# Streamed key and value weight pieces: one load per row piece instead of two half loads

## The chip, the cores and the metric

The kernel runs on one core of a Trainium2 chip. The metric is the device time of one execution in microseconds: the median of three runs before is 3,844.53 us (3,838.34 to 3,846.89). The profiled execution has a span of 3,837.5 us, from which all times below are taken. Engines are called PE (TensorE, matrix products; its weight loads are a row of their own, PEld), DVE (VectorE), ACT (ScalarE), POOL (GpSimd) and SP (SyncE, which here only issues transfers). Transfers from SP share one load queue, q1; those from POOL go through q0.

## The reference

Four layers, A B A B, act on `x` of 2048 rows and 640 columns, all bf16. Only layer A matters here; it is a recurrence over segments:

```python
for s in range(n_seg):                       # 64 segments of 32 rows
    h = concatenate([mem, xs])               # 8 memory rows + 32 rows of x
    q, k, v = h @ Wq, h @ Wk, h @ Wv         # 640 -> 32 heads x 192 each
    p = softmax(where(mask, q @ k.T * scale, -1e9))
    o = (p @ v) @ Wo                         # 6144 -> 640
    mem = o[:8]                              # goes into the next segment
    outs.append(o[8:])
```

The segments must run one after the other, since the first 8 output rows of one are the first 8 input rows of the next. Layer B is a linear attention with softmax features, and each layer adds its result to `x`. Layer A runs twice, so there are 128 segments.

## The kernel before, in words

**Where the weights are.** Each of Wq, Wk and Wv is 640 x 6144. It is cut in 4 rounds of 1536 columns (8 heads each; `PW = 1536`) and in 5 contraction blocks of 128 rows (`KC = 5`), which makes 20 pieces of 128 partitions x 1536 columns, 384 KB each. Not all of it fits in the on-chip memory beside the output weight Wo. So of each matrix 17 places are held: rounds 1 and 2 whole, two blocks of rounds 0 and 3 each for good (`res`), and three places (`SLOTS`, `slot`) that blocks 2, 3 and 4 of rounds 0 and 3 use in turn. The rounds of a segment run 0, 1, 2, 3 in even segments and 3, 2, 1, 0 in odd ones (`rounds`), so what the last round of a segment used is what the first round of the next one needs. Per segment each slot is loaded once. Wo has the same trouble: rounds 1 and 2 stay in `wo_mid`, rounds 0 and 3 share `wo_end`, which is loaded with six pieces of 320 KB in each segment (`load_wo`, line 625; they come from `wo_rows`, a copy of these rounds with contiguous rows).

**A segment.** `A_chain` (lines 811 to 1095) writes out by hand the order of all instructions (a manual schedule). For each of the four rounds there are query, key and value projections (`project`, line 867, matmuls of line 882, 20 for each projection), scores (lines 919, 924), softmax sums (985), the attention product (`attend`, 932), and the round of the output projection (`wo_round`, 48 matmuls of line 958, which reads the six Wo pieces one after the other, 8 matmuls each). The four rounds' work is interleaved: the projections of a round come ahead of the attention of the one before it. The output projection of the last round ends the segment; lines 1091 and 1092 turn its first rows into the columns `hT` that the next segment's first matmuls read.

**When the slots are loaded.** In the first round (`n == 0`) `project` starts with the blocks in the slots, and right after the four matmuls of such a block it puts the load of the last round's block in the slot:

```python
b = (i + KC - ns) % KC if n == 0 else i
...
if n == 0 and b >= KC - ns:
    load_slot(m, order[NR - 1], b)
```

The load has to wait until those matmuls have read the slot, and its data is used in the last round, block by block. Queries come first, then keys, then values. The Wo pieces are issued after the first `wo_round` of the segment has read `wo_end`.

**How the matmuls read a piece.** Matmuls of one block come in four, one for each group `g` of 32 output partitions. For keys and queries each of the four reads columns from all over the piece, in strides. For values each reads 384 neighbouring columns, in the order of groups 0, 2, 1, 3 of the columns, so the first and third lie in the first half of the piece and the second and fourth in the second half.

**Queue.** SP issues all these loads in the program's order and waits in front of each for what it needs; a later load can't pass an earlier one. Eight semaphores count the landings of SP's loads in turn, so each load also waits until the eighth load before it has landed. POOL issues small transfers at the same time: the tails of keys and queries (`load_kqb`, line 853) and values (`extra_v`, line 865) that were worked out ahead, and results (lines 834, 849, 951).

**Ahead of the chain.** `A_pre` works out those tails for all segments; there `load_matrix` calls `load_slot` with `whole=True`, so these loads are whole rows before the change too.

Of the kernel before, what the change touches and what calls it, by code (L numbers as in the profile page):

```python
# [112 lines left out]
class Kernel:  # L113
# [456 lines left out]
    def layer_A(self, xn_dram, at_dram, li, x_raw=None):  # L570
        nc, tc = self.nc, self.tc
        KC, NSEG = self.KC, self.NSEG
        dram = self.dram
        NR = 4
        PW = 1536
        self.kqb_d = dram.tile([NSEG, P, NR, 192], BF16, name=f"kqb{li}")
        self.vb_d = dram.tile([NSEG, NR, 2, 8, 896], BF16, name=f"vb{li}")
        self.otb_d = dram.tile([NSEG, P, 384], BF16, name=f"otb{li}")
        wview = self.wview
        wov = self.A_Wo.rearrange("h d m -> (h d) m").rearrange("(c p) m -> p c m", p=P)  # L580
        low = self.view(0, LATE)
        at = LATE
        res, slot = {}, {}
        for r in (3, 2):
            for m in "KQV":
                for b in range(KC - (SLOTS[m] if r == 3 else 0)):
                    res[m, r, b] = low[:, len(res) * PW:len(res) * PW + PW]
        assert len(res) * PW * 2 == LATE
        for m, r, b in [(m, 0, b) for m in "KQV" for b in range(KC - SLOTS[m])] + \
                [(m, None, b) for m in "KQV" for b in range(KC - SLOTS[m], KC)] + [(m, 1, b) for m in "KQV" for b in range(KC)]:  # L590
            v = self.view(at, 2 * PW)
            at += 2 * PW
            if r is None:
                slot[m, b] = v
            else:
                res[m, r, b] = v
        holds = {}
        wo_mid = self.view(at, 24 * 1280)
        wo_end = self.view(at + 24 * 1280, 12 * 1280)
        assert at + 36 * 1280 == ARENA  # L600
        unread = set(res)

        def load_slot(m, r, b, whole=False):
            if holds.get((m, b)) != r:
                holds[m, b] = r
                w = PW if whole or m == "Q" else PW // 2
                for h in range(0, PW, w):
                    nc.sync.dma_start(out=slot[m, b][:, h:h + w], in_=wview[m][:, b, PW * r + h:PW * r + h + w])

        def load_matrix(m, r):  # L610
            for b in range(KC):
                if (m, r, b) in unread:
                    unread.remove((m, r, b))
                    nc.sync.dma_start(out=res[m, r, b], in_=wview[m][:, b, PW * r:PW * r + PW])
                elif (m, r, b) not in res:
                    load_slot(m, r, b, True)

        early = {(0, 5), (2, 4), (2, 5), (1, 0), (1, 1), (1, 2), (1, 3)}

        def load_wo(r, into=None, part=range(6)):  # L620
            t = into if into is not None else wo_end[:, :] if r in (0, 3) else wo_mid[:, 7680 * (r - 1):7680 * r]
            for k in part:
                tk = t[:, 1280 * k:1280 * k + 1280]
                if r in (0, 3):
                    self.last_load = nc.sync.dma_start(out=tk, in_=self.wo_rows[r // 3, :, 1280 * k:1280 * k + 1280])
                else:
                    nc.sync.dma_start(out=tk.rearrange("p (c m) -> p c m", m=640),
                                      in_=wov[:, 12 * r + 2 * k:12 * r + 2 * k + 2, :])

        def piece(m, r, b):  # L630
            assert (m, r, b) in res or holds[m, b] == r
            return res[m, r, b] if (m, r, b) in res else slot[m, b]

        def lay_out_wo():
            if li == 0:
                self.wo_rows = dram.tile([2, P, 7680], BF16, name="wo_rows")
                for i, r in enumerate((0, 3)):
                    nc.scalar.dma_start(out=self.wo_rows[i].rearrange("p (c m) -> p c m", m=640),
                                        in_=wov[:, 12 * r:12 * r + 12, :])

        def early_wo():
            for r in (0, 2, 1):
                load_wo(r, part=[k for k in range(6) if (r, k) in early])

        def late_wo(r):
            load_wo(r, part=[k for k in range(6) if (r, k) not in early])

        self.A_pre(xn_dram, li, load_matrix, piece, wo_mid, wo_end, lay_out_wo, early_wo, x_raw)
        self.A_chain(xn_dram, at_dram, li, load_slot, piece, load_wo, late_wo, wo_mid, wo_end, low)
        self.post_args = at_dram, wo_mid, wo_end, low  # L650

# [510 lines left out]
```

## Time and profile before

| what | before |
|---|---|
| median of three runs | 3,844.53 us |
| span of the profiled run | 3,837.5 us |
| PE busy | 3,549.1 us (92%) |
| DVE, ACT, POOL busy | 61%, 54%, 43% |
| loads of Wk and Wv of 192 KB | 768 and 768 |
| of 384 KB | 46 and 46 |
| q1: packets, MB, share of the 16 DMA engines | 449,194, 805.76, 61.0% |
| q0: the same | 68,288, 88.95, 7.9% |
| instruction queue of PE (q8) | 551 packets, 9.03 MB, 1.0% |
| DMA share in the two chains (300 to 1,600 and 2,200 to 3,500 us) | 0.82 and 0.83 |

The first chain lies between about 210 and 1,640 us, the second between about 2,115 and 3,525 us; a segment takes 21 to 23 us. A DMA share of 0.82 is a mean over a segment that has stretches with full engines and stretches with nearly none. A packet of q1 carries one row of one load: 1,536 B for the half loads, 3,072 B for the whole ones, 2,560 B for Wo, and 4 B for each engine's report that its part has landed. The matmuls' ends in the profile are modelled, so idle time between two matmuls is a lower bound of a delay; the distance between their starts is not modelled.

### The profile page before, as it was taken

How to read it: one execution, taken by the hardware profiler on the slowest of the kernel's cores; microseconds unless marked ns; L12 is line 12 of the kernel's file. 1: busy time of each engine (PE TensorE's matmuls, PEld its weight loads, DVE VectorE, ACT ScalarE, POOL GpSimd, SP SyncE). 2: the span in 40 equal slices, each digit the busy share in tenths (PEclk: the TensorE clock that was granted, in tenths of full speed). 3: DMA queues.
4: the chain of work that ended last, by engine and by line, in shares of the span. 5: the costliest groups of instructions: out<-in, count | busy, mean ns of one | idle time of the engine just before them, and what ended most of it. 6: DMA issues, size and time to landing. Idle time of an engine off the chain costs nothing. (4 is left out here: it accounts for less than half of the span.)

```text
span 3837.5 us, 167748 instructions
## 1 busy us (share of the span) xinstructions
PE 3549.1 (92%) x70296; PEld 2239.0 (58%) x70312; DVE 2328.4 (61%) x6038; ACT 2071.6 (54%) x5285; POOL 1665.3 (43%) x4367
## 2 busy tenths in 40 slices
PE   7889999999999999889899899999999999999898
PEld 5655665555656656555467556566556665565453
DVE  3546666666666666645643566666666666664465
ACT  2245655555656666536432466566556665664453
POOL 2435454444545545440242454454444555453300
PEclk9999999999999999989899999999999999999899
DMA  9787888888878888850367888888878888888200
GB/s 325 247 274 257 284 282 270 274 271 271 283 271 282 286 278 284 286 154 1 116 235 205 287 279 275 274 274 287 276 257 287 280 290 276 272 295 297 76 1 28
DMA packets 587906, 935.20 MB, mean 244 GB/s; under 512 B 147322, under 2 KB 402826, under 8 KB 587146
## 3 DMA queue, kind: packets, MB, share of 16 engines
q1 hardware_dynamic: 449194, 805.76, 61.0%
q0 software_dynamic: 68288, 88.95, 7.9%
q10 hardware_dynamic: 69664, 29.76, 2.9%
q8 instruction: 551, 9.03, 1.0%
q14 instruction: 209, 1.71, 0.1%
HBM read 855.97 MB, written 72.09 MB: 242 GB/s over the span
## 5 line engine op out<-in xcount | busy, mean ns | idle before, releaser
L882 PE MATMUL ps_qk<-arena,hT 128*32 128x384 bf16 x20480 | 1001.6, 328 | 26.4 <-DMA arena<-in_A_Wk_dram 10.1
L882 PEld LDWEIGHTS <-hT 128*32 128x32 bf16 x30720 | 740.2, 97 | 475.4 <-DVE hT L1092 58.8
L892 ACT ACTIVATE raw<-ps_qk 128x384 bf16<-128x384 f32 x1024 | 502.0, 490 | 442.6 <-PE ps_s L985 250.1
L958 PE MATMUL ps_w<-arena,OT 128*32 128x160 bf16 x24576 | 550.5, 234 | 74.2 <-issue 48.4
L865 POOL DMA_DIRECT2D Vp<-vb x512 | 258.7, 505 | 675.4 <-PE ps_o L932 467.9
L958 PEld LDWEIGHTS <-OT 128*32 128x32 bf16 x24576 | 436.1, 97 | 191.1 <-issue 96.5
L882 PE MATMUL ps_v<-arena,hT 128*32 128x384 bf16 x10240 | 538.5, 330 | 1.9 <-issue 1.1
L897 DVE STREAM_TRANSPOSE KT<-raw 128x384 bf16<-128x384 bf16 x512 | 296.1, 578 | 199.6 <-ACT raw L892 195.6
L900 DVE STREAM_TRANSPOSE QT<-raw 128x256 bf16<-128x256 bf16 x512 | 227.9, 445 | 268.1 <-ACT raw L892 240.9
L853 POOL DMA_DIRECT2D kqb<-kqb x512 | 290.1, 567 | 165.7 <-POOL KT L861 148.4
L913 DVE CAST Vp<-ps_v 64x384 bf16<-64x384 f32 x512 | 286.2, 559 | 102.5 <-ACT Vp L911 88.1
L951 POOL DMA_DIRECT2D otb<-otb x512 | 282.5, 552 | 140.3 <-DVE otb L947 101.0
L911 ACT ACTIVATE Vp<-ps_v 64x384 bf16<-64x384 f32 x512 | 246.1, 481 | 157.5 <-PE ps_v L882 121.8
L938 DVE CAST OT<-ps_o 128x192 bf16<-128x192 f32 x512 | 182.9, 357 | 219.5 <-PE ps_o L932 201.2
L932 PEld LDWEIGHTS <-Vp 80*128 80x128 bf16 x4096 | 181.9, 99 | 197.0 <-issue 130.7
L992 DVE TENSOR_TENSOR E<-E,ps_s 80x320 bf16<-80x320 bf16 x512 | 247.5, 483 | 73.5 <-ACT ps_s L991 69.3
L971 ACT ACTIVATE E<-ps_s 80x320 bf16<-80x320 f32 x512 | 221.5, 433 | 110.6 <-PE ps_s L924 97.1
L932 PE MATMUL ps_o<-E,Vp 80*128 80x80 bf16 x4096 | 234.3, 202 | 34.6 <-DMA Vp<-vb 6.9
L924 PE MATMUL ps_s<-QT,KT 128*80 128x80 bf16 (+1 forms) x3072 | 233.9, 213 | 20.6 <-DVE KT L897 12.5
L858 POOL COPY QT<-kqb 128x64 bf16<-128x64 bf16 x512 | 125.7, 246 | 283.5 <-PE ps_s L924 280.2
L937 ACT ACTIVATE OT<-ps_o 128x192 bf16<-128x192 f32 x512 | 167.7, 328 | 141.4 <-PE ps_o L932 141.3
L965 PE MATMUL ps_idle<-arena,ident 128*128 128x384 bf16 x1024 | 233.4, 330 | 3.3 <-issue 3.3
(147 smaller groups left out, 5336.2 us busy)
## 6 DMA issues: line engine op xcount, KB each, us to landing
arena<-wo_rows SPq DMA_DIRECT2D x792, 320.0 KB, 5.9
arena<-in_A_Wq_dram SPq DMA_DIRECT2D x430, 384.0 KB, 4.5
arena<-in_A_Wk_dram SPq DMA_DIRECT2D x768, 192.0 KB, 5.6
arena<-in_A_Wv_dram SPq DMA_DIRECT2D x768, 192.0 KB, 5.1
kqb<-arena ACTq DMA_DIRECT2D x16, 1536.0 KB, 8.7
kqb<-kqb POOLq DMA_DIRECT2D x512, 48.0 KB, 5.0
arena<-in_A_Wk_dram SPq DMA_DIRECT2D x46, 384.0 KB, 7.5
arena<-in_A_Wv_dram SPq DMA_DIRECT2D x46, 384.0 KB, 7.7
```

What stands on the lines that cost most here:

```text
L853: nc.gpsimd.dma_start(out=kqb[:], in_=self.kqb_d[s, :, r, :])
L865: nc.gpsimd.dma_start(out=Vs[n % 2][64:80, :], in_=self.vb_d[s, r].rearrange("g t f -> (g t) f"))
L882: nc.tensor.matmul(o[32 * g:32 * g + 32, 0:384], lhsT=hT[:, b, :], rhs=rhs, start=(i == 0), stop=(i == KC - 1), tile_position=(0, 32 * g), ...
L892: nc.scalar.activation(out=raw[:], in_=ps[:, 0:384], func=ACT.Copy)
L897: nc.vector.transpose(out=KT[:, :, 0:64], in_=raw[:, :].rearrange("p (c j) -> p c j", j=64))
L911: nc.scalar.activation(out=o, in_=i, func=ACT.Copy)
L913: nc.vector.tensor_copy(out=o, in_=i)
L924: nc.tensor.matmul(S[0:80, c0:c0 + 80 * (q1 - q0)], lhsT=KT[:, 3 * x + i, :], rhs=QT[:, x, q0:q1, :], start=False, stop=(x == 1 and i == 2 ...
L932: nc.tensor.matmul(O[x][:, 80 * i:80 * i + 80], lhsT=Vs[n % 2][0:80, 448 * x + k:448 * x + k + 128], rhs=E[0:80, 160 * x + 80 * e:160 * x ...
L951: nc.gpsimd.dma_start(out=self.otb_d[s, :, 96 * r:96 * r + 96], in_=otb[:, :, :].rearrange("p c t -> p (c t)"))
L958: nc.tensor.matmul(W[32 * g:32 * g + 32, 0:160], lhsT=OT[:, c, q:q + 32], rhs=w[:, 640 * i + 160 * g:640 * i + 160 * g + 160], start=(firs ...
L992: nc.vector.tensor_tensor(out=E[0:80, 0:320], in0=E[0:80, 0:320], in1=rc, op=ALU.mult)
```

## The change

Before, the slot loads of keys and values in the chain are split in two halves of 768 columns, each a transfer of its own; those of queries are whole. The change takes the split away: each piece of keys and values is one transfer of 128 rows x 1536 columns. The aim is fewer transfers with longer contiguous rows for the same bytes.

```diff
-        def load_slot(m, r, b, whole=False):
+        def load_slot(m, r, b):
             if holds.get((m, b)) != r:
                 holds[m, b] = r
-                w = PW if whole or m == "Q" else PW // 2
-                for h in range(0, PW, w):
-                    nc.sync.dma_start(out=slot[m, b][:, h:h + w], in_=wview[m][:, b, PW * r + h:PW * r + h + w])
+                nc.sync.dma_start(out=slot[m, b], in_=wview[m][:, b, PW * r:PW * r + PW])
 
         def load_matrix(m, r):
             for b in range(KC):
...
                 elif (m, r, b) not in res:
-                    load_slot(m, r, b, True)
+                    load_slot(m, r, b)
```

Lines after 606 of the changed kernel carry numbers lower by two than before.

## The prediction, made before the changed kernel ran

> **What bounds the kernel now.** I read the page for the split of the time, then the stretches of both chains, then the waits of TensorE, then one segment closely. Two chains of 64 segments (layers 0 and 2) fill about 2 x 1,410 of the 3,838 us; the changed transfers run only there (and in the short passes ahead, where they are whole rows already). Parts 1 and 6 of the page:
>
> ```profile
> PE 3549.1 (92%) x70296; PEld 2239.0 (58%) x70312; DVE 2328.4 (61%) x6038; ACT 2071.6 (54%) x5285; POOL 1665.3 (43%) x4367
> ...
> arena<-wo_rows SPq DMA_DIRECT2D x792, 320.0 KB, 5.9
> arena<-in_A_Wq_dram SPq DMA_DIRECT2D x430, 384.0 KB, 4.5
> arena<-in_A_Wk_dram SPq DMA_DIRECT2D x768, 192.0 KB, 5.6
> arena<-in_A_Wv_dram SPq DMA_DIRECT2D x768, 192.0 KB, 5.1
> ```
>
> TensorE is at 92%, so only what it still waits for can be won. 768 + 768 half loads over 128 segments are 6 + 6 a segment, beside 3 query pieces and 6 pieces of the output weight. A 192 KB load that takes 5.6 us to land has others ahead of it. Busy time by stretches of one segment (997.98 to 1019.38 us; the last two columns are DMA share and GB/s):
>
> ```profile
> 1000.50:1003.00 2.50, 2.50 (x58) 1.43 (x47) 2.05 (x6) 1.53 (x4) 0.61 (x4) 1.00 1.01 392
> 1003.50:1007.00 3.50, 3.41 (x76) 2.15 (x68) 2.75 (x7) 2.75 (x8) 1.56 (x5) 1.00 1.06 379
> 1007.00:1010.00 3.00, 3.00 (x100) 2.10 (x97) 1.84 (x5) 1.81 (x5) 1.49 (x4) 1.00 0.92 301
> 1011.00:1016.00 5.00, 4.76 (x138) 3.00 (x131) 3.33 (x11) 3.17 (x10) 3.08 (x11) 1.00 1.00 349
> 1016.00:1017.50 1.50, 1.18 (x23) 0.85 (x23) 0.68 (x3) 0.46 (x2) 1.14 (x4) 1.00 0.56 195
> 1017.50:1020.50 3.00, 2.90 (x78) 1.71 (x80) 2.04 (x7) 1.45 (x6) 0.22 (x1) 1.00 0.14 38
> ```
>
> The DMA engines are full (share about 1) from 2 us after the segment's start until some 3 us before its end; the stretches are queries, then keys and values, then output weight. So each segment's stream is a fixed amount of DMA work that must fit between the release of the first slot and the last round of the output projection. What TensorE waits for (waits of TensorE, and what idled before line 958):
>
> ```profile
> PE ps_w L958 <- issue: 48.4, 52, 1.8
> PE ps_w L958 <- DMA arena<-wo_rows: 24.1, 48, 1.7
> PE ps_qk L882 <- DMA arena<-in_A_Wk_dram: 10.1, 6, 4.5
> PE ps_o L932 <- DMA Vp<-vb: 6.9, 16, 0.8
> ```
>
> Late key pieces are six cases, values none. The wait that recurs is for the last output-weight pieces, which stand last in the queue. A segment that shows it, TensorE only:
>
> ```profile
> 928.86 0.80 PE L958 MATMUL ps_w<-arena,OT 128*32 128x160 bf16 x32
> 930.15 0.32 PE L958 MATMUL ps_w<-arena,OT 128*32 128x160 bf16 x8 [0.49 <-DMA arena<-wo_rows]
> 932.16 0.32 PE L958 MATMUL ps_w<-arena,OT 128*32 128x160 bf16 x8 [1.69 <-DMA arena<-wo_rows]
> ```
>
> The round halts after 32 and 40 of its 48 matmuls: the fifth and sixth of the six pieces are late. The 24.1 us count idle time after a matmul's modelled end only. From the starts of those two matmuls in the 124 segments inside the two chains, less the usual spacing, I get 45.2 us: the 48 idles plus about 0.2 us hidden in each by the modelled duration, plus delays under 0.2 us. The other recurring loss, "issue", halts at places that differ from segment to segment. In the packet records 16 KB fetches on the instruction queue stand about 1.3 us before them: TensorE has run out of instructions. Segments average 21.81 us, the quickest are 20.85: 119 us in all above the floor.
>
> **What the Trainium skill says.** DMA: Bandwidth & Descriptors, Why small descriptors are slow: a fixed overhead per packet, plus 32 bytes of descriptor metadata. The trace agrees: a 1,536 B packet of the load queue takes 65 ns at the median, a 3,072 B packet 121, so a row costs 130 ns in two packets and 121 in one; a 4 B completion packet costs 9. The same page, Specifications, puts line rate at 512 B and up, by which nothing were to be gained; the trace shows 7% between 1,536 and 3,072 B, and I follow the trace. Its Queues, rings and completion order: each engine turns between queues packet by packet, so longer packets make other queues wait longer; no trace here shows that apart. Runtime: NRT & Kernel Launch, Instruction fetch mechanics: 16 KiB refills, mostly hidden; the refills are there, hidden they are not always.
>
> **The change part by part.** *Removed:* 3 + 3 of the 12 half loads a segment. Each of the 16 engines carries 8 of a piece's 128 rows: 6 x 8 = 48 rows a segment. Saved per engine: 48 x (130 - 121) = 432 ns, plus 6 completions x 9 = 54 ns: 0.49 us. That is with the medians. By the means in the loaded stretches (71 to 73 ns against 127 to 136) a row costs 142 to 146 against about 132, so 48 x 12 + 54 = 0.63 us at the upper end. The lower end, 0.3 us, is for the slowest engine, which alone decides the landing: in the last 2 us of a stream only a few engines still work, with gaps. I take 0.5 us.
>
> *Issue:* SyncE issues 15 loads a segment for 21, at 0.33 to 0.42 us each. I cost this at nothing: SyncE waits 1,189.8 us for the first matmuls of the next segment (line 608 for ps_qk).
>
> *Order:* the eight load semaphores are used in turn, so a load waits for the landing of the eighth before it. Now that holds value loads back to 5.8 to 9.6 us after the segment's start (medians); with 9 loads ahead of the output weight, they go out by about 4. The engines have work either way, so this moves queueing, not landing. The output weight can't go earlier: it overwrites what the round of line 958 reads until 10.07 us, and goes out at 10.28 now. By then values are still landing (last at 14.4, then about 13.9), so its six pieces follow on without a gap and land 0.5 us earlier.
>
> *Waits added:* a value matmul of the first two head groups that read the first half now waits for the whole piece; keys read both halves anyway. Third key pieces land at 10.8 and are read after 12.6; value pieces land by 14.4 and are read from 15.5 (medians). Half a piece is 0.5 us: it lies inside both margins, cost nothing. TensorE, VectorE, ScalarE and GpSimd carry the same instructions in the same order.
>
> *Sum:* moving the last landing 0.5 us ahead shortens each delay by up to 0.5 us. Applied to the 124 delays one by one (ten are over 1 us, about sixty under 0.1), that saves 29.1 us of 45.2; with 0.3 us 21.8, with 0.8 us 36.3. Times 128/124: 30. I take off 4 us because a halt for data lets instruction fetch catch up, and some refills will show instead, and add 2 us for late keys: 28 us. 3,844.5 - 28 = 3,816 us.
>
> **The rivals.**
> *Instruction fetch takes the place of the wait.* For it: the "issue" halts come in the same dense stretch, nearly 0.5 us a segment. Against: they come before the wait as often as within it. Also in this case: the slowest engine is held by refills and small transfers, not by row count. Saving 0 to 8 us: 3,840.
> *More than the stream's wait.* The engines idle earlier in the tail, so refills and the small transfers land faster, and the full 45 us plus part of the fetch halts go: 45 + about 15 = 60: 3,785. For it: the halts cluster while the DMA is loaded by the output weight. Against: early rounds run under equal load almost without halts.
> *Slower.* Key and value packets of 121 ns instead of 65 stand before each packet of the small GpSimd transfers: attention tails (48 KB, 9 packets an engine) could take 9 x 56 = 0.5 us longer, and refills wait for longer packets. For it: ps_o already waits for Vp 16 times, so its margin is near nothing in one of eight segments. If every one of the 128 lost 0.15 us net of the gain: + 20, 3,864. Against: the tail at risk goes out while the output weight begins, whose packets don't change; the 48 KB tails are fetched two rounds ahead.
>
> **How the numbers follow.** Forecast 0.58, fetch takes over 0.18, more 0.13, slower 0.11. The forecast's own spread, with 0.3 to 0.8 us, is 3,809 to 3,824 by the same sum; measured times of before spread by 8 us. Reaching into "more" on one side and over "fetch takes over" on the other: 3,796 to 3,848. Faster by over 0.2% (under 3,837): the forecast, "more", and a few hundredths of "fetch takes over": 0.76. Within 0.2%: 0.13. Slower: 0.11.
>
> **What would show it.** Right: q1 loses 98,304 packets, and its share falls by some 1.5 points or more; key and value loads are 384 KB; the last output weight lands about 0.5 us earlier; PE ps_w for wo_rows falls from 24.1 us to under 12; "issue" stays near 48. Wrong: the landings don't move though packets fell (slowest engine); "issue" grows by what wo_rows loses (fetch); ps_o for Vp or ps_s for KT grows above 20 us (slower). A lower granted clock in the chains, now 0.99, would also break it.

## The result, and the profile after

The changed kernel takes 3,892.57 us (median of four runs, 3,888.04 to 3,899.86) against 3,845.38 us before in the same comparison: ratio 1.0128, 95% interval 1.0106 to 1.0150. It is slower, by 47 us, where 28 us faster was forecast.

The page after, parts 1, 3 and 6. Lines of the kernel after line 606 are lower by two than before.

```profile
PE 3565.1 (92%) x70296; PEld 2257.0 (58%) x70312; DVE 2329.2 (60%) x6038; ACT 2066.2 (53%) x5285; POOL 1665.0 (43%) x4367
...
q1 hardware_dynamic: 338602, 805.71, 57.7%
...
q8 instruction: 551, 9.03, 1.0%
...
arena<-wo_rows SPq DMA_DIRECT2D x792, 320.0 KB, 6.4
arena<-in_A_Wk_dram SPq DMA_DIRECT2D x430, 384.0 KB, 6.4
arena<-in_A_Wq_dram SPq DMA_DIRECT2D x430, 384.0 KB, 4.6
arena<-in_A_Wv_dram SPq DMA_DIRECT2D x430, 384.0 KB, 8.4
```

The transfers did what they were meant to do: the same bytes with 110,592 packets fewer (98,304 data rows and 12,288 completions of 4 B), and q1's share falls from 61.0% to 57.7%. The last output-weight piece lands 19.6 us into a segment instead of 20.3 (medians of 124 segments). But value loads now take 8.4 us from issue to landing, where halves took 5.1: they stand in a longer queue. Waits of TensorE after:

```profile
PE ps_w L956 <- issue: 79.8, 87, 2.7
...
PE ps_o L930 <- issue: 10.2, 9, 1.6
...
PE ps_qk L880 <- issue: 8.9, 19, 1.1
PE ps_v L880 <- issue: 8.7, 14, 1.2
...
PE ps_w L956 <- DMA arena<-wo_rows: 7.5, 8, 1.8
...
PE ps_o L930 <- DMA Vp<-vb: 0.6, 2, 0.4
```

The halts for wo_rows fell from 24.1 us in 48 cases to 7.5 in 8, as forecast. "issue" rose from 48.4 to 79.8 ahead of ps_w alone, and stands now ahead of projections and attention too, where it was 0.3 to 5.4 us. One such halt, in the segment from 888.9 to 913.8 us, TensorE only:

```profile
906.45 0.30 PE L956 MATMUL ps_w<-arena,OT 128*32 128x160 bf16 x5
908.67 1.53 PE L956 MATMUL ps_w<-arena,OT 128*32 128x160 bf16 x43 [1.92 <-issue]
910.13 0.82 PE L963 MATMUL ps_idle<-arena,ident 128*128 128x384 bf16 x2
```

The round stops after its fifth matmul, though its weights are the resident ones, and the view names no input that is late. The next view is the busy time in three stretches around it (the last three columns are the granted clock, DMA share and GB/s):

```profile
905.00:908.00 3.00, 1.75 (x36) 0.91 (x34) 1.94 (x7) 2.01 (x5) 1.36 (x5) 1.00 0.65 233
908.00:912.00 4.00, 3.33 (x56) 2.32 (x56) 0.60 (x3) 0.43 (x2) 1.32 (x3) 0.61 0.14 34
912.00:916.00 4.00, 3.92 (x102) 2.33 (x104) 2.02 (x8) 1.71 (x6) 1.90 (x4) 0.97 0.25 45
```

After this halt the granted clock is 0.61 for 4 us, so the halt was paid for a second time. The records show ten periods of 3.4 us at half clock inside segments after the change, two before. I estimate that 3.4 us at half clock do the work of 1.7, so eight more cost at most 14 us.

**What "issue" is here.** TensorE's instructions come in packets of 16 KB on the instruction queue, 551 for 141,012 instructions: 256 each. I number TensorE's instructions in order of start and list the places where one starts over 0.4 us after the one before, in 124 segments, by number modulo 256:

```
                          before          after
gaps over 0.4 us          123, 119.8 us   181, 179.1 us
  at numbers 184 to 194    71,  78.2 us   163, 167.0 us
  elsewhere                52,  41.6 us    18,  12.1 us
```

Eleven of 256 places hold 163 of 181 gaps: the limits between two 16 KB pages. And the halts there end when a packet arrives: 162 of the 163 end 2.2 to 2.8 us after the start of a packet on the instruction queue, of the 18 elsewhere one does. The others are mostly the halts for the output weight. So the change took 29.5 us of those away and added 88.8 us at page limits. The net, 59 us, is what the segments show to within overlaps: their mean went from 21.81 to 22.23 us, 124 x 0.42 = 52 us.

A page's packet starts some time after TensorE enters the page before it, the *refill delay* below, and its instructions run no sooner than 2.2 us after that start (the least of all pages, in both kernels). So a page is late when delay + 2.2 us is more than TensorE needs for 256 instructions. That is 4.6 to 6.4 us for most pages, and 3.9 us at the least, where output rounds fall close together (a round's 96 take 0.85 us). The medians of the delay by the time at which the page before is entered:

```
us in the segment   4-6   6-8   8-10  10-12  12-14  14-16  16-18  18-20
before              2.8   2.0   1.6   2.2    2.4    3.4    1.8    1.2
after               3.0   2.6   2.5   3.5    3.6    2.7    1.1    1.2
```

From 6 to 14 us, the key and value stretch, the delay grew by 0.6 to 1.3 us. Halts at page limits that begin 6 to 18 us into a segment went from 29 to 133, later ones from 42 to 30. This is the step to explain.

### The profile page after: what moved, and what is told of

Its sections match the earlier page's. It is cut to its first block, busy times and chain, and to the rows that moved or that the text cites. A ratio compares the mean times of both kernels' runs of the same rounds, so it can differ in the third digit from the quotient of the medians.

```text
span 3887.3 us, 166590 instructions
## 1 busy us (share of the span) xinstructions
PE 3565.1 (92%) x70296; PEld 2257.0 (58%) x70312; DVE 2329.2 (60%) x6038; ACT 2066.2 (53%) x5285; POOL 1665.0 (43%) x4367
## 3 DMA queue, kind: packets, MB, share of 16 engines
q1 hardware_dynamic: 338602, 805.71, 57.7%
## 5 line engine op out<-in xcount | busy, mean ns | idle before, releaser
L880 PEld LDWEIGHTS <-hT 128*32 128x32 bf16 x30720 | 748.6, 97 | 501.3 <-DVE hT L1090 65.1
L956 PE MATMUL ps_w<-arena,OT 128*32 128x160 bf16 x24576 | 552.9, 236 | 88.3 <-issue 79.8
L844 ACT ACTIVATE Vp<-ps_w 32x160 bf16<-32x160 f32 x512 | 150.7, 294 | 207.0 <-DVE wt L1089 200.2
```

The source lines that it names most:

```text
L880: nc.tensor.matmul(o[32 * g:32 * g + 32, 0:384], lhsT=hT[:, b, :], rhs=rhs, start=(i == 0), stop=(i == KC - 1), tile_position=(0, 32 * g), ...
L956: nc.tensor.matmul(W[32 * g:32 * g + 32, 0:160], lhsT=OT[:, c, q:q + 32], rhs=w[:, 640 * i + 160 * g:640 * i + 160 * g + 160], start=(firs ...
```

## The experiments

Theory 1: longer *packets* hold up a refill. Theory 2: the *depth* of the load queue does. Eight semaphores allow eight loads in flight; with whole rows these are twice the bytes, and value loads go out by 3.6 to 5.0 us instead of 5.8 to 9.6. Theory 3: the refills got no slower, the halts for the output weight had *hidden* them. A last question is whether late refills cost time by themselves at all. Times are medians; each trace is of one run. It lies within 7 us of the median but for the change aligned (24 us below), the output weight paced (11 below), and the even-odd, both-paced and aligned keys-only kernels (12 to 15 above).

**Long packets at the old depth, first try.** 64-partition halves:

```diff
-                for h in range(0, PW, w):
-                    nc.sync.dma_start(out=slot[m, b][:, h:h + w], in_=wview[m][:, b, PW * r + h:PW * r + h + w])
+                for h in range(0, P, w):    # w = P // 2
+                    nc.sync.dma_start(out=slot[m, b][h:h + w, :], in_=wview[m][h:h + w, b, PW * r:PW * r + PW])
```

> Key and value pieces in two loads each as before the change, but the halves are 64 partitions of 3,072 B rows instead of 128 partitions of 1,536 B rows: long packets, with the old number of loads and so the old depth of the queue. Measured after the change: TensorE runs out of instructions more often (issue before ps_w 79.8 us against 48.4), and a 16 KB instruction refill starts about 3.0 us after TensorE enters the page before, in the stretch from 6 to 14 us of a segment, against 2.0 before. Theory 1 (packet length: the refill stands behind load packets of 121 ns instead of 65): like the changed kernel, 3,880 to 3,895 us, issue near 80, that delay near 3 us. Theory 2 (depth: value loads go out 4 us earlier, more bytes stand ahead of the refill): delay near 2 us, issue near 48, and since the stream is still 0.4 us shorter 3,815 to 3,845 us. Theory 3 (exposure: refills got no slower, the halts for Wo hid them): like the changed kernel in time, but with the delay near 2 us.

Measured 4,261.76 us, ratio 1.1079 (1.1052 to 1.1105). A 3,072 B row took 172 ns at the median instead of 121, the stream grew by 3.6 us a segment, and halts for wo_rows are 105.7 us. This run tells nothing of the theories, only that such halves are costly here.

**Long packets at the old depth, second try.** Even and odd partitions instead:

```diff
...
+                    nc.sync.dma_start(out=slot[m, b][h:P:n, :], in_=wview[m][h:P:n, b, PW * r:PW * r + PW])    # n = 2
```

> Again long rows with the old number of loads, since the rows of the 64-partition halves took 172 ns and blurred that run: each key and value piece in two loads, even partitions and odd partitions, rows of 3,072 B. If the rows take about 121 ns now: the depth theory (a refill of TensorE's instructions starts later the more load bytes are outstanding; 1.1 us with none, about 2.0 at 1 MB, 3 at 1.3 MB and more) expects the refill delay as before the change, near 2 us from 6 to 14 us of a segment, issue before ps_w under 55 us, the shorter stream kept, 3,805 to 3,840 us. The packet theory expects the changed kernel's numbers: delay 3 us, issue near 80, 3,880 to 3,900 us. If the rows are slow again, it tells nothing of this.

Rows take 121 ns again, and the refill delay from 6 to 14 us is 1.3 to 1.4 us, shorter than before the change: packets of 3,072 B alone do not make a refill late. Issue ahead of ps_w is 37.3 us. But the time is 3,915.55 us, 1.0183 (1.0145 to 1.0220), not the 3,805 to 3,840 expected: the last output-weight piece lands at 21.2 us instead of 20.3, and halts for wo_rows are 85.7 us. The test is not clean either: these loads leave the engines partly idle. The mean DMA share from 8 to 16 us of a segment is 0.89 to 0.96, where the kernel before has 0.98 to 1.04. Why is open.

**Short packets, deep queue.** Two loads of three half pieces per matrix:

```diff
...
+                elif b == KC - 1:
+                    for h in range(0, PW, w):
+                        nc.sync.dma_start(out=slots3[m][:, :, h:h + w], in_=wview[m][:, KC - 3:KC, PW * r + h:PW * r + h + w])
```

> Short packets with a deep queue: the three slots of keys and of values are filled by two loads of three half pieces each (128 partitions x 3 rows of 1,536 B, 576 KB), issued after the third slot is read. 13 loads a segment, so all value loads are queued early and more bytes than after the change are ahead of a refill. Theory 1: like the kernel before, 3,835 to 3,860 us, refill delay about 2 us, issue near 50. Theory 2: like the changed kernel or worse, 3,880 us or more, delay 3 us or more, issue 80 or more. Theory 3: like the kernel before.

3,927.16 us, 1.0198 (1.0166 to 1.0231), with the short packets of before (65 ns). Delay 2.8 to 3.9 us from 6 to 14 us, 192 gaps at page limits. TensorE's waits in this kernel:

```profile
PE ps_w L963 <- issue: 91.2, 95, 2.2
PE ps_w L963 <- DMA arena<-wo_rows: 6.1, 9, 1.5
```

Theory 2 as expected, and theories 1 and 3 fall for this kernel. Pages sorted by the load bytes that are issued but not yet started when the page before is entered, with the median delay in us (a dash: no pages):

```
MB outstanding            0-0.1  0.4-0.8  0.8-1.2  1.2-1.6  2.0-2.4
before                    1.13   1.61     2.03     2.72     -
after                     1.11   1.67     2.39     3.30     2.89
short packets, deep       1.15   1.71     2.75     3.63     2.80
```

The delay rises with the bytes ahead and stays near 3 us from 1.2 MB on, and the length of a row doesn't sort the three kernels: short packets in a deep queue have the longest delays. But bytes are not the whole account. At 1.2 to 1.6 MB the three medians stand in the order of the size of one load (192, 384 and 576 KB), and in the even-odd kernel, from 6 to 14 us with 1.0 to 1.4 MB outstanding, it is 1.4 us against 2.0 to 2.4 before. The size of one load was not tested apart from the number in flight.

**Shorter stream.** The chain loads five of six output-weight pieces and leaves the sixth out:

```diff
-                            load_wo(order[L])
+                            load_wo(order[L], part=range(5))
```

> The kernel before, but in the chain only five of the six Wo pieces are loaded anew in each segment (the sixth keeps the data of the other round, so the output rows are not the reference's): the stream is about 1 us shorter with nothing else changed, so the halts for Wo go. Theories 1 and 2: the refill delay stays near 2 us in the key and value stretch, issue stays at 35 to 55 us, the gain is kept: 3,795 to 3,815 us. Theory 3: issue takes over what the halts for Wo lose and more, 75 us or more, 3,845 us or slower.

3,787.34 us, 0.9848 (0.9817 to 0.9880):

```profile
PE ps_w L958 <- issue: 17.8, 29, 2.0
PE ps_w L958 <- DMA arena<-wo_rows: 12.0, 25, 1.1
```

The halts for the output weight are halved, and late refills don't come out in their place: they become fewer. But the sixth piece's bytes are missing too, and the delay from 14 to 16 us falls from 3.4 to 2.5 us, so this run doesn't say what exposure alone is worth. Theory 3 falls as an account of the change by its own premise, since the refills did get slower.

**Shorter output-weight packets.** 2 x 1,280 B instead of 2,560 B:

```diff
...
+                    two = lambda v: v.rearrange("p (c m) -> p c m", m=640)[:, 4 * (k // 2) + k % 2:4 * (k // 2) + k % 2 + 3:2, :]
+                    self.last_load = nc.sync.dma_start(out=two(t), in_=two(self.wo_rows[r // 3]))
```

> The kernel before, but each of the six Wo loads of a segment takes two rows of 1,280 B that are not neighbours (steps k and k + 2) instead of one row of 2,560 B: same bytes, loads and order of loads, shorter packets (55 against 102 ns), stream about 48 x 8 ns = 0.4 us longer per segment. Theory 1: the refill delay in the Wo stretch (12 to 16 us of a segment) falls from 2.4 to 3.4 us to under 2.4, issue falls from 48 to under 30, the halts for Wo grow by about 0.3 us a segment: 3,830 to 3,865 us. Theories 2 and 3: delay and issue as before or (3) less issue only by the longer halts, 3,860 to 3,890 us.

3,882.42 us, 1.0100 (1.0065 to 1.0134). The delay at 14 to 16 us stays at 3.4 us with packets half as long, issue is 43.8; halts for wo_rows double to 51.8. Theory 1 falls again. The stream's length counts the other way round: the last piece lands 0.5 us later.

**Depth set by hand.** A tiny load behind each key and value load takes one of the eight semaphores (in the kernel it is a helper, written out here):

```diff
                 nc.sync.dma_start(out=slot[m, b], in_=wview[m][:, b, PW * r:PW * r + PW])
+                if m != "Q":
+                    nc.sync.dma_start(out=self.pad[:, 4 * j:4 * j + 4], in_=self.B_wo[0:16, 4 * j:4 * j + 4])
```

> The changed kernel, whole rows, with a tiny load (16 partitions x 8 B into an unused place) behind each key and value load of the chain. The tiny loads take turns on the eight load semaphores, so again only about four pieces are outstanding instead of eight: rows of 3,072 B with the old depth. Depth theory: refill delay near 2 us from 6 to 14 us, issue before ps_w at or under 50 us, output weight still some 0.4 us earlier than before the change: 3,805 to 3,840 us, faster than or like before. Packet theory: like the changed kernel, 3,880 us or more, since its packets are the same.

The refill part came: delays of 1.5 to 2.4 us from 6 to 14 us with whole rows, as before the change. From 6 to 10 us the engines are full here (share 1.01), and the delays are 2.3 and 1.5 us against 2.6 and 2.5 with the same loads in a deeper queue; this is the clearest sign for depth. The time didn't come: 3,889.19 us, 1.0119 (1.0094 to 1.0143), with the last piece landing at 21.0 us and halts for wo_rows of 51.7 us beside issue of 58.1. With the tiny loads behind the output weight too, and with those alone in the kernel before:

> As the run with paced rows, and a tiny load behind each of the six Wo loads as well: at most four loads outstanding in the whole stream but for the queries. Depth theory: the refill delay in the Wo stretch (14 to 16 us) falls from 3.4 to about 2.5 us, issue under 35 us, 3,790 to 3,830 us; if four loads are too few to keep the slowest engine fed, halts for wo_rows come back instead and eat that. Packet theory: 3,880 us or more.

> The kernel before the change with a tiny load behind each Wo load: only the depth in the Wo stretch changes. Depth theory: refill delay at 14 to 16 us falls from 3.4 to about 2.5 us, issue before ps_w from 48 to under 35 us, halts for wo_rows as before or a little more: 3,820 to 3,845 us. Packet theory: issue and delay unchanged, 3,845 to 3,860 us.

Both got rid of most late refills (26 and 21 halts at page limits are left of 71) and lost time: 3,928.42 us, 1.0226 (1.0194 to 1.0258), and 3,869.40 us, 1.0066 (1.0043 to 1.0090). The second, whose only difference from the kernel before is the depth in the output-weight stretch:

```profile
PE ps_w L968 <- DMA arena<-wo_rows: 92.9, 142, 2.6
PE ps_w L968 <- issue: 2.2, 8, 0.5
```

Set against before (24.1 and 48.4), issue is gone and the wait for data has taken its place: the last piece lands at 21.0 us instead of 20.3 (21.4 in the other). So the queue's depth had two sides here: deep, the stream was quicker and the refills late; shallow, the reverse. With few loads in flight the engines run partly dry: in the second kernel the mean DMA share from 12 to 18 us is 0.91 to 0.97, where the kernel before has 0.98 to 0.99.

**Only the page limits moved.** Loads untouched; very short matmuls (32 columns of weights, 8 of data) make a segment 1,024 instructions long on average instead of 1,011, so that its limits stay in place, and some ahead of each chain choose where:

```diff
+            short(idle, 56 if li == 0 else 43)
             for s in range(NSEG):
...
                 wo_round(W, order[L], OT, False, True)
-                keep_busy(idle, 3)
+                keep_busy(idle, 2)
+                short(idle, 7 + s % 2)
```

> The kernel before, with the page limits of TensorE's instruction stream put in fixed places. A segment is 1,011 instructions; one of the filling matmuls at its end is replaced by 7 or 8 very short ones in turn, so that it is 1,024 on average, four refills of 256, and 56 (first chain) and 43 (second chain) short ones ahead of the chains put the limits at about 0.9, 6.7, 11.9 and 17.1 us of each segment, where the refill measured before would always come in time. No load changes. If late refills cost time by themselves, issue before ps_w falls from 48 to under 10 us and segments average 21.1 to 21.5 us instead of 21.81: 3,775 to 3,820 us; the halts for wo_rows stay or grow to 60 us. If the halts called issue were only time that the halts for Wo would take anyway: 3,835 to 3,860 us.

> The control for the aligned run: the same short matmuls, but 21 and 43 of them ahead of the chains, which put the page limits at about 2.4, 8.7, 13.8 and 17.7 us, where the third refill of a segment is asked for in the stretch with the longest delay (3.4 us) and its page is used up soonest. If late refills cost time: about one late refill of 1 to 2 us per segment, issue 100 us or more, 3,880 to 3,960 us. If they cost nothing: like the aligned run.

Aligned 3,808.32 us, 0.9899 (0.9882 to 0.9916); misaligned 3,871.20 us, 1.0052 (1.0033 to 1.0070). First the aligned, then the misaligned kernel:

```profile
PE ps_w L958 <- DMA arena<-wo_rows: 39.3, 95, 1.4
...
PE ps_w L958 <- issue: 0.7, 3, 0.4
```

```profile
PE ps_w L958 <- issue: 58.8, 72, 2.1
PE ps_w L958 <- DMA arena<-wo_rows: 44.2, 97, 2.0
```

One late page against 72, from 35 short matmuls ahead of the first chain (by that the limits in the second chain, too, lie at 2.2, 8.5, 13.3 and about 18 us instead of 0.7, 6.7, 11.5 and 17.1). The two differ by 63 us with the same loads and the same work in each segment. The halts for wo_rows differ by 5 us only. This shows that late refills cost time by themselves. The misaligned one was expected still slower; its delay at the third limit was 2.2 to 2.5 us, not 3.4.

**The change, aligned.** The same edit on whole rows, with 86 and 43 short matmuls:

> The changed kernel (whole rows) aligned in the same way, with 86 and 43 short matmuls ahead of the chains: limits at about 5.4, 10.2, 15.7 and 20.0 us, the best places for the delays measured with whole rows; two of the four refills are still late by about 0.3 us by that count. If the loss of the change is the late refills, it goes: 3,785 to 3,825 us, at or under the aligned kernel before plus 20 us, with halts for wo_rows under 15 us and issue under 40. If the change costs by another way (packets, clock), it stays 40 us or more above the aligned kernel before.

3,874.00 us, 1.0062 (1.0042 to 1.0083): better than the change alone, by half its loss, but far from the expected 3,785 to 3,825. Halts for wo_rows are 5.3 us, and:

```profile
PE ps_v L880 <- issue: 64.2, 111, 1.7
```

The pages that begin at about 10.9 and 16.9 us were late, 56 and 82 of the 141 times in all; the refill delay at the earlier limit was 3.2 to 3.6 us. By my reckoning from the delays measured with whole rows of both matrices, no place has all four pages in time.

**One part alone.** Keys whole and values in halves, first as it is:

```diff
-                w = PW if whole or m == "Q" else PW // 2
+                w = PW if whole or m != "V" else PW // 2
```

> One part alone: keys in whole rows, values in halves as before; 18 loads a segment. The depth theory expects the queue depth and so the refill delay between the two kernels in the stretch from 6 to 12 us, late refills between 70 and 165, the output weight about 0.3 us earlier than before: 3,850 to 3,880 us. If depth mattered only through the values, which are the loads held back most before: like before, 3,830 to 3,850 us.

3,846.93 us, 1.0001 (0.9987 to 1.0015): no difference. The time is that of the second expectation, but the rest is that of the first: halts for wo_rows are 7.8 us, the last piece lands 0.5 us earlier, issue ahead of ps_w is 53.8, and 119 halts stand at page limits, between the 71 and 163 of the two kernels. The gain and the loss cancel. Then each part alone with aligned limits (for values `m != "K"`):

> Keys in whole rows, values in halves, with the page limits aligned as in the aligned kernel before (about 0.8, 6.7, 11.8 and 17.1 us). The refill delays of the keys-only run (2.7 us at 6 to 8, 2.8 at 10 to 12, 1.6 at 16 to 18) leave these refills in time. If the forecast step was right in itself (a stream 0.4 us shorter takes the halts for wo_rows) and only late refills undid it: halts for wo_rows under 15 us against 39.3 in the aligned kernel before, issue under 10 us, 3,775 to 3,800 us. If whole rows cost time in another way: 3,808 us or more.

> Values in whole rows, keys in halves, aligned in the same way. Values are the loads that the eight semaphores held back; with whole rows they go out early, and the queue is deep at the limit at 11.9 us, whose refill the page up to 17.1 us needs. If this depth does the harm: refill delay at 12 us of 3 us or more, 20 to 60 late refills, 3,800 to 3,830 us, slower than keys alone. If the harm needs both: like keys alone, 3,775 to 3,800 us.

Keys alone 3,805.86 us, 0.9899 (0.9877 to 0.9921); values alone 3,781.80 us, 0.9825 (0.9805 to 0.9846). I had expected values alone to be the slower one. With limits in these places whole key rows bring nothing against the aligned kernel before (0.9899 both times), and whole value rows bring a gain. Waits of keys alone, then of values alone:

```profile
PE ps_o L932 <- issue: 28.4, 53, 1.6
PE ps_w L958 <- issue: 24.9, 51, 0.8
...
PE ps_w L958 <- DMA arena<-wo_rows: 7.7, 12, 1.5
```

```profile
PE ps_w L958 <- issue: 19.1, 34, 1.7
PE ps_w L958 <- DMA arena<-wo_rows: 9.6, 26, 0.8
```

Both cut the halts for wo_rows to a fourth or less of the aligned kernel's 39.3. With keys alone the refills were late after all, so its time fell between its two expectations. With whole key rows only 6 loads instead of 9 precede the first value load, so value loads go out at 4.4 to 8.0 us, and the delay at the second and third limits is 2.4 to 3.0 us. With halved keys the value loads wait until 6.0 to 7.5 us, and the delay at the second limit is 1.0 to 1.8, at the third 2.4 to 3.0 as well; 101 halts stand at page limits with keys alone, about half of them each at the third and the fourth; 37 with values alone, 33 of them at the fourth. Values alone in whole rows with aligned limits is the best kernel of this study: 0.9825 against before, and quicker than the aligned kernel before by more than both intervals. Values alone without alignment were not run.

## Why the prediction was wrong

*The bound and the stream* were right in kind. The chains wait for the last output-weight pieces, and whole rows make these land earlier: 0.8 us at the median (20.36 to 19.57), where I took 0.5 with 0.63 as the upper end. Halts for wo_rows fell to 7.5 us, "under 12". The other recurring loss was the larger one already, though: 78.2 us of long gaps at page limits against 41.6 elsewhere.

*The 29.1 us* of the sum came near the 29.5 us of long gaps that went away off the page limits, but by luck. The 45.2 us behind it come out of the trace when 3 ns are taken for the usual distance between two starts. That is the median of all; at every fourth matmul, where the two pieces begin, it is 59. With 59 the delays are 33.3 us, and 0.5 us earlier would have saved 20.4. Of these 33.3 us 0.9 are left after the change. A base too large and a shift too small made up for each other.

*The order step failed.* It said that value loads going out 4 us earlier "moves queueing, not landing". It does, and that was taken as costing nothing. The step named what a deeper queue does to the loads, and not who else gets its data by the same engines: TensorE's instructions. Refills asked for from 6 to 14 us waited 0.6 to 1.3 us longer, and long gaps at page limits grew by 88.8 us. The sum had 4 us in that place. The step was also wrong that the output weight can't go earlier: its first piece needs only the round's first 8 matmuls to be done. With the value loads out of the way it went out at 9.60 us instead of 10.28 (medians), before the round's last matmul in each of the 124 segments (until then in a third of them), which deepens the queue from there on.

*The 4 us* stood for another mechanism, exposure of refills that a halt had hidden. No run prices it apart. In the five-piece run issue fell from 48.4 to 17.8 us while the halts were halved, but fewer bytes were in the queue as well.

*The rivals.* "Instruction fetch takes the place of the wait" named the right wait, with the wrong reason and size: it was held to end at 3,840 at worst because nothing was thought to make the refills slower. "Slower" had refills among its reasons, by longer packets; the short-packet run has the late refills without them, and the paced run has whole rows without the longer delay. That speaks for depth; a part that goes with the size of one load is not excluded. The other reason under "Slower", tails of values late, didn't come: ps_o waits for Vp 0.6 us instead of 6.9.

*The Trainium skill.* "Mostly hidden", of refills (Runtime: NRT & Kernel Launch, Instruction fetch mechanics), I doubted in the forecast but didn't price. The trace of before held the price: 71 of its 123 long gaps stood at page limits, and the refill delay already ran from 1.1 us in an idle stretch to 3.4 us in a loaded one. By DMA: Bandwidth & Descriptors, Queues, rings and completion order, engines turn between queues packet by packet; a packet there is 9 to 17 descriptors as a rule, so the one-row packets of the profile, on which the forecast leaned, need not be its unit. Either way, that alone would not let the depth of one queue delay another. Here the delay grows with it, and the measurement decides. By what mechanism bytes in one queue delay a packet in another stays open.

*The half clock* after some halts had no cost in the forecast, which named a lower clock only as a sign of being wrong; by the estimate above it is at most 14 us of the loss.

## What to carry to other kernels

When transfers are merged, ask what the bound on loads in flight counts: if it counts loads and not bytes, merging deepens the queue, and what else the same engines fetch may come later. Here the instruction refills did, by 0.6 to 1.3 us, and value tails that POOL issued 6 to 8 us into a segment took 5.6 us to land instead of 4.9. Look for "issue" waits at every 256th instruction, compare the time that a page takes with the refill delay under load, and try the place of the page limits before tuning the loads. A gain in a stream is worth what the next wait in the same stretch leaves of it, so price that wait under the new traffic and not under the old.

## What the runs showed of the hardware that was not expected

- A page limit's place is worth 63 us of 3,850 here: 0.9899 aligned, 1.0052 misaligned, with the same loads.
- The refill delay of TensorE's instructions rises from 1.1 us with an almost empty load queue to some 3 us with 1.2 MB and more outstanding (2.7 to 3.6 us in three kernels), with rows of 65 and of 121 ns.
- Loads to 64 neighbouring partitions took 172 ns per 3,072 B row (median) against 121 ns to even or odd partitions or to all 128; the kernel was 10.8% slower.
- Fewer loads in flight made the same bytes land later: 21.0 us instead of 20.3 for the last piece, with only tiny loads added; the mean DMA share from 12 to 18 us fell from 0.98 and more to 0.91 to 0.97.
- In the changed kernel 8 of 9 pauses of over 2.1 us between two matmul starts inside a segment were followed by 3.4 us at half the granted clock, and none of 54 between 1.0 and 1.8 us. It is no rule: in the kernel before one of four such long pauses was followed by it.
